# A linear-attention and MLP kernel on one core: 1 KB-run loads on one queue, casts on chip, streamed weights, a zero-padded last chunk and a ring of token tiles

## The chip, the cores and the metric

The kernel runs on one core of a Trainium2 chip. The core has TensorE (PE, matmuls and transposes into PSUM), VectorE (DVE), ScalarE (ACT), GpSimd (POOL) and SyncE (SP, which here issues DMAs). Sixteen DMA engines move data between HBM and SBUF. Each engine takes its own instructions in their order and waits on semaphores for the others. The metric is the device time of one execution in microseconds (us); lower is better.

## What is computed

Eight batches, eight heads, 576 tokens, head size 64. Attention without a score matrix, then a two-layer MLP over all 4608 tokens with the heads side by side (512 columns), all f32 in and out:

```python
q_s = softmax(q, axis=-1)                       # over the 64 values of a head
k_s = softmax(k, axis=2)                        # over the 576 tokens
kv  = einsum('bhsd,bhse->bhde', k_s, v)
x   = einsum('bhsd,bhde->bhse', q_s, kv)        # -> (4608, 512)
h   = x @ w_in                                  # (512, 2048)
out = maximum(0.01 * h, h) @ w_out              # (2048, 512)
```

## The kernel before

The Tile framework takes the program as it is written, gives each engine its list of instructions (in an order that its scheduler works out) and puts in the waits. All matmuls are bf16 with f32 sums.

**Loads.** `emit_loads(b)` cuts the 576 tokens of a batch into chunks of 128, 128, 128, 128 and 64, one token on each partition. For each chunk SP loads q and k (L107, L111) into `qk_sb` in f32: of each token and head one run of 64 values, 256 bytes. GpSimd loads v (L119) and casts it to bf16 on the way, two DMAs a chunk, into `v_sb`, with a column of ones beside it. GpSimd also loads and casts the weights: `w_in` in 16 pieces behind batch 0's v (L88), `w_out` in 8 behind batch 1's (L96).

**Attention of a batch** is a list of pieces. A prep piece for each chunk: ScalarE's exponential of q and k together (`qke_sb`, L135), DVE's row sums, reciprocal and scaling of q (`qsum` L138, `qrecip` L140, `qn_sb` L143). A transpose piece for each chunk: four PE transposes (`psum_qt`, L163) and DVE's copy into `qT_stage` (L171). Four `kv` pieces, one for each pair of heads: five matmuls (`pkv`, L186), a reciprocal (L194) and two scalings into the block-diagonal `kd_all` (L195, L202). Four out pieces: two matmuls of 288 columns (`po`, L218) and ScalarE's copies into `xT` (L225), one large tile for all 4608 tokens.

**MLP.** `emit_moe(t, pieces)` works on 512 tokens, nine token tiles in all. First 16 groups of four matmuls (`ph`, L251), each evicted by ScalarE with the leaky ReLU into `g_sb` (L259). Then four groups of 16 matmuls (`pout`, L277), each copied by DVE into `out_sb` (L285) and stored by SP (L287). After each group one attention piece of the next batch is put in, so that tile t carries the attention of batch t + 1 (tiles 0 to 6; 7 and 8 carry none). Token tile 0 lies within batch 0, tile 1 within batches 0 and 1. PSUM has 8 banks: six for `psB_pool` (all but `pout`), two for `pout`.

Of the kernel before, what the change touches and what calls it, by code (L numbers as in the profile page):

```python
# [19 lines left out]
def kernel(  # L21
# [22 lines left out]
    HEADS_PER_G = 2  # L44

    n_full = S // P
    rem = S - n_full * P
    chunk_sizes = [P] * n_full + ([rem] if rem else [])
    n_chunks = len(chunk_sizes)
# [43 lines left out]
    def emit_w_out_loads():  # L93
        w_out_r = moe_w_out.rearrange("(fb f) o -> f fb o", f=P)
        for fb0 in range(0, NF, 2):
            nc.gpsimd.dma_start(  # L96
                out=w_out_sb[:, fb0 : fb0 + 2, :], in_=w_out_r[:, fb0 : fb0 + 2, :]
            )

    xT = xT_pool.tile([P, NB, T], BF16)  # L100

    def emit_loads(b):
        st = {"qk": [], "v": [], "qke": {}, "qn": {}}
        for ci, cs in enumerate(chunk_sizes):
            s0 = ci * P
            qk_sb = qk_pool.tile([P, 2, H, D], FP32, name="qk_sb")
            nc.sync.dma_start(  # L107
                out=qk_sb[:cs, 0],
                in_=q[b, :, s0 : s0 + cs, :].rearrange("h s d -> s h d"),
            )  # L110
            nc.sync.dma_start(  # L111
                out=qk_sb[:cs, 1],
                in_=k[b, :, s0 : s0 + cs, :].rearrange("h s d -> s h d"),
            )

            v_sb = v_pool.tile([P, NG, 132], BF16, name="v_sb")
            v_src = v[b, :, s0 : s0 + cs, :].rearrange("(g hp) s d -> s g hp d", hp=2)
            for hp in range(HEADS_PER_G):
                nc.gpsimd.dma_start(  # L119
                    out=v_sb[:cs, :, hp * D : (hp + 1) * D],  # L120
                    in_=v_src[:, :, hp, :],
                )
# [219 lines left out]
```

## Time and profile before

| | us |
|---|---|
| median of 3 runs (348.08 to 349.3) | 349.28 |
| profiled execution, from its first to its last instruction | 346.2 |
| PE busy in it | 285.7 |
| ScalarE busy | 143.9 |
| DVE busy | 121.2 |
| GpSimd busy | 79.6 |

The profile is one execution. Its span leaves out what lies around the instructions; the run's time holds it. A busy time adds up the instructions of an engine. Matmuls are pipelined: one of 512 columns is listed with some 380 ns, but the next starts 216 ns after it. In the view by stage, a row is the stage, its length, the busy time (and instructions) of PE, of PE's weight loads, of DVE, ACT and POOL, then the TensorE clock as a share of full speed, the mean number of DMA engines' queues busy as a share of the 16 engines, and the GB/s that they moved. A row of a timeline is start, length, engine, line, operation, written tile and read tiles, number of instructions, and in brackets how long the engine had been idle and what ended that. In the DMA view a queue's row is packets, MB, and the packets' time as a share of 16 engines over the stretch. In the view by group a row is line, engine, operation, tiles, shapes and count, then busy us in all and mean ns of one, then idle time before them and its causes.

### The profile page before, as it was taken

The page shows a single profiled execution, that of the slowest core. Times are in us where ns is not written, and L with a number is a line of the kernel's source. Part 1 is how long each engine was busy: PE and PEld are TensorE (multiplying, and loading weights), DVE is VectorE, ACT ScalarE, POOL GpSimd, SP SyncE. Part 2 cuts the span into 40 slices and gives each one's busy share as a digit, 9 for nine tenths or more (in the row PEclk, how much of TensorE's full clock was granted, in tenths as well). Part 3 has the DMA queues.
Part 4 walks back from the last instruction along what each step waited for, and adds up shares of the span by engine and source line. Part 5 has one row for each costly group of instructions (what it writes and reads, how often), then busy time and mean ns, then how long its engine had stood idle before and what let it go on. Part 6 is the DMA issues. An engine that isn't in the chain of part 4 may idle for free.

```text
span 346.2 us, 4150 instructions
## 1 busy us (share of the span) xinstructions
PE 285.7 (83%) x1506; PEld 138.5 (40%) x1536; DVE 121.2 (35%) x292; ACT 143.9 (42%) x250; POOL 79.6 (23%) x158
## 2 busy tenths in 40 slices
PE   0203000999999999999999999999999999999995
PEld 0102000444445445544554454455445544444442
DVE  0523213476424822561465247225313210011011
ACT  2212111679155716753581457166225405503600
POOL 8667746208101700440071012000000000000000
PEclk9999999999999999999999999999999999999999
DMA  9999999999997992398089204100110021011011
GB/s 159 198 196 170 198 192 174 174 199 158 186 241 112 165 245 57 28 218 218 1 97 228 79 2 54 62 31 0 61 62 0 2 80 42 2 61 62 2 55 66
DMA packets 122837, 37.51 MB, mean 108 GB/s; under 512 B 114112, under 2 KB 118208, under 8 KB 122816
## 3 DMA queue, kind: packets, MB, share of 16 engines
q1 hardware_dynamic: 80192, 28.32, 38.0%
q0 software_dynamic: 42624, 8.92, 28.7%
q8 instruction: 12, 0.20, 0.2%
q14 instruction: 9, 0.07, 0.1%
HBM read 36.70 MB, written 9.44 MB: 133 GB/s over the span
## 4 chain that ended last, share of the span: by engine, by line
PE 78%; SPq 11%; DMA 8%; issue 1%; ACT 1%; DVE 0%; ACTq 0%
PE pout L277 36%; PE ph L251 35%; DMA qk_sb<-in_k_dram 8%; SPq L107 6%; SPq L111 5%; PE pkv L186 3%; PE psum_qt L163 2%; PE po L218 2%; ACT qke_sb L135 1%; DVE out_sb L285 0%; ACT g_sb L259 0%; ACTq L135 0%
## 5 line engine op out<-in xcount | busy, mean ns | idle before, releaser
L251 PE MATMUL ph<-xT,w_in_sb 128*128 128x512 bf16 x555 | 137.5, 382 | 2.0 <-ACT g_sb L259 0.7
L259 ACT ACTIVATE g_sb<-ph 128x512 bf16<-128x512 f32 x144 | 85.6, 598 | 113.4 <-PE ph L251 113.3
L277 PE MATMUL pout<-w_out_sb,g_sb 128*128 128x512 bf16 x567 | 127.6, 379 | 0.5
L119 POOL DMA_DIRECT2D v_sb<-in_v_dram x80 | 58.3, 749 | 113.1 <-PE pkv L186 102.2
L277 PEld LDWEIGHTS <-g_sb 128*128 128x128 bf16 x576 | 56.3, 98 | 64.1
L251 PEld LDWEIGHTS <-w_in_sb 128*128 128x128 bf16 x576 | 52.7, 98 | 55.7 <-issue 2.2
L135 ACT ACTIVATE qke_sb<-qk_sb 128x1024 bf16<-128x1024 f32 (+1 forms) x40 | 40.8, 1062 | 46.3 <-DMA qk_sb<-in_k_dram 46.3
L285 DVE COPY out_sb<-pout 128x512 f32<-128x512 f32 x36 | 24.6, 684 | 100.0 <-PE pout L277 83.2
L138 DVE TENSOR_REDUCE qsum<-qke_sb 128x8 f32<-128x512 bf16 (+1 forms) x40 | 26.8, 669 | 54.4 <-ACT qke_sb L135 54.2
L163 PE MATMUL psum_qt<-ident,qn_sb 128*128 128x128 bf16 (+1 forms) x160 | 15.7, 224 | 26.9 <-DVE qn_sb L143 26.9
L218 PE MATMUL po<-qT_stage,kd_all 128*128 128x288 bf16 x64 | 13.9, 304 | 27.1 <-DVE kd_all L202 27.0
L171 DVE COPY qT_stage<-psum_qt 128x512 bf16<-128x512 bf16 (+1 forms) x40 | 15.7, 396 | 43.8 <-PE psum_qt L163 43.4
L225 ACT CAST xT<-po 128x288 bf16<-128x288 f32 x64 | 22.2, 412 | 20.0 <-PE po L218 20.0
L143 DVE TENSOR_TENSOR qn_sb<-qke_sb,qrecip 128x512 bf16<-128x512 bf16 (+1 forms) x40 | 27.4, 686 | 0.8
L163 PEld LDWEIGHTS <-qn_sb 128*128 128x128 bf16 (+1 forms) x160 | 11.4, 101 | 37.5 <-DVE qn_sb L143 28.0
L218 PEld LDWEIGHTS <-kd_all 128*128 128x128 bf16 x64 | 6.1, 100 | 35.2 <-issue 27.2
L186 PE MATMUL pkv<-v_sb,qke_sb 128*128 128x129 bf16 (+1 forms) x160 | 18.5, 232 | 0.0
L186 PEld LDWEIGHTS <-qke_sb 128*128 128x128 bf16 (+1 forms) x160 | 13.0, 100 | 10.8 <-issue 0.8
L194 DVE RECIPROCAL krecip<-pkv 128x1 f32<-128x1 f32 x32 | 5.4, 168 | 20.0 <-PE pkv L186 20.0
L88 POOL DMA_DIRECT2D w_in_sb<-in_moe_w_in_dram x16 | 8.5, 535 | 5.0 <-DMA w_in_sb<-in_moe_w_in_dram 2.4
L202 DVE TENSOR_SCALAR kd_all<-pkv,krecip 64x64 bf16<-64x64 f32 x32 | 9.3, 291 | 0.5
L195 DVE TENSOR_SCALAR kd_all<-pkv,krecip 64x64 bf16<-64x64 f32 x32 | 8.8, 276 | 1.6
(12 smaller groups left out, 26.9 us busy)
## 6 DMA issues: line engine op xcount, KB each, us to landing
out_dram<-out_sb SPq DMA_DIRECT2D x36, 256.0 KB, 2.0
qk_sb<-in_q_dram SPq DMA_DIRECT2D x32, 256.0 KB, 5.2
qk_sb<-in_k_dram SPq DMA_DIRECT2D x32, 256.0 KB, 6.2
v_sb<-in_v_dram POOLq DMA_DIRECT2D x64, 64.0 KB, 6.1
w_in_sb<-in_moe_w_in_dram POOLq DMA_DIRECT2D x16, 128.0 KB, 6.5
w_out_sb<-in_moe_w_out_dram POOLq DMA_DIRECT2D x8, 256.0 KB, 10.2
qk_sb<-in_q_dram SPq DMA_DIRECT2D x8, 128.0 KB, 4.6
qk_sb<-in_k_dram SPq DMA_DIRECT2D x8, 128.0 KB, 4.5
```

Of the source, the lines that this page charges most:

```text
L119: nc.gpsimd.dma_start(out=v_sb[:cs, :, hp * D : (hp + 1) * D], in_=v_src[:, :, hp, :],)
L135: nc.scalar.activation(out=qke_sb[:cs], in_=qk_sb[:cs], func=AF.Exp)
L138: nc.vector.reduce_sum(out=qsum[:cs], in_=qke_sb[:cs, 0], axis=AX.X)
L143: nc.vector.tensor_tensor(out=qn_sb[:cs], in0=qke_sb[:cs, 0], in1=qrecip[:cs].to_broadcast([cs, H, D]), op=ALU.mult,)
L163: nc.tensor.matmul(psum_qt[:, j, 0:cs], lhsT=qn_flat[:cs, j * P : (j + 1) * P], rhs=ident[:cs, :cs], is_transpose=True, start=(j == 0), st ...
L186: nc.tensor.matmul(pkv[:, 0:129], lhsT=ke_flat[:cs, g * P : (g + 1) * P], rhs=st["v"][ci][:cs, g, 0:129], start=(ci == 0), stop=(ci == n_c ...
L218: nc.tensor.matmul(po[:, 0:width], lhsT=kd_all[:, g, :], rhs=qT_stage[:, g, lo : lo + width], start=True, stop=True,)
L225: nc.scalar.copy(out=xT[:, g, b * S + lo : b * S + lo + width], in_=po[:, 0:width])
L251: nc.tensor.matmul(ph, lhsT=w_in_sb[:, cb, j * P : (j + 1) * P], rhs=xT[:, cb, t0 : t0 + TT], start=(cb == 0), stop=(cb == NB - 1),)
L259: nc.scalar.activation(out=g_sb[:, j, :], in_=ph, func=AF.Prelu, alpha=LEAKY_SLOPE)
L277: nc.tensor.matmul(pout, lhsT=g_sb[:, j, tsub * P : (tsub + 1) * P], rhs=w_out_sb[:, j, :], start=(j == 0), stop=(j == NF - 1),)
L285: nc.vector.tensor_copy(out=out_sb, in_=pout)
```

## The change

- **Loads.** SP issues every load, all in f32. A batch's first 512 tokens are dealt out four neighbours to a partition (R = 4), so that a partition reads of each head one run of 4 x 64 values, 1 KB (L95); the last 64 tokens (REM) go in runs of 256 bytes to 64 partitions (L99). q, k and v each have one staging tile of a ring of 8 (`ld`). Token order inside the 512 is undone when ScalarE writes `xT`.
- **Casts.** The weights come in quarters of 1 MB through the same ring, and DVE casts them (L121, L126). v is cast by ScalarE for batch 0 and by DVE for the others (L156, L157).
- **Order.** Batch 0 in halves, `w_in`, three quarters of `w_out`, batch 1, the last quarter of `w_out`, then batch 2 and on.
- **Zero-padded last chunk.** The buffers for exponentials and v (`qe`, `ke`, `vb`, two of each) are fixed tiles; their unused 64 partitions of the fifth chunk are set to zero once, so that every matmul has 128 rows. GpSimd does nothing but build the identity.
- **Attention.** Exponentials and softmax by halves of the heads; two pairs of heads to a `pkv` tile; `po` as 512 + 64 columns, the 64 copied by DVE. Batch 0 multiplies k and v ahead of the transposes.
- **Tiles.** `xT` is a ring of three token tiles. All PSUM tiles share 8 banks. Tile 0 takes no piece during `ph`, and its four `pout` sums run side by side, each weight row of `w_out` used for all four; pieces come in from its ninth row on.

```diff
-    xT_pool = ctx.enter_context(tc.tile_pool(name="xT", bufs=1))
-    qk_pool = ctx.enter_context(tc.tile_pool(name="qk", bufs=8))
...
+    ld_pool = ctx.enter_context(tc.tile_pool(name="ld", bufs=8))
+    xT_pool = ctx.enter_context(tc.tile_pool(name="xT", bufs=3))
+    ps_pool = ctx.enter_context(tc.tile_pool(name="ps", bufs=8, space=bass.MemoryType.PSUM))
...
+    def load_rows(dst, src, b, h0, h1):
+        nc.sync.dma_start(
+            out=dst[:, h0:h1, 0 : R * D],
+            in_=src[b, h0:h1, 0:MAIN, :].rearrange("h (p r) d -> p h (r d)", r=R),
+        )
+        nc.sync.dma_start(
+            out=dst[0:REM, h0:h1, R * D : NR * D],
+            in_=src[b, h0:h1, MAIN:S, :].rearrange("h p d -> p h d"),
+        )
...
-                nc.gpsimd.dma_start(
-                    out=w_in_sb[:, cb, fq * FQ : (fq + 1) * FQ],
-                    in_=w_in_r[:, cb, fq * FQ : (fq + 1) * FQ],
-                )
+    def emit_w_in(i):
+        stg = ld_pool.tile([P, NB, FQ], FP32, name="w_in_ld", tag="ld")
+        nc.sync.dma_start(out=stg, in_=w_in_r[:, :, i * FQ : (i + 1) * FQ])
+        nc.vector.tensor_copy(out=w_in_sb[:, :, i * FQ : (i + 1) * FQ], in_=stg)
...
+            copy = nc.scalar.copy if b == 0 else nc.vector.tensor_copy
+            copy(out=vb[:, 0:R, h0:h1, 0:D], in_=rhd(st["v"][:, h0:h1, 0 : R * D], R))
+            copy(out=vb[0:REM, R, h0:h1, 0:D], in_=st["v"][0:REM, h0:h1, R * D : NR * D])
...
+        if b == 0:
+            front = [make_exp(st, b, "q", 0), make_exp(st, b, "q", 1)]
+            front += [make_qnorm(st, b, 0), make_qnorm(st, b, 1)]
+            for hf in range(2):
+                front += [make_exp(st, b, "k", hf), make_vcast(st, b, hf), make_kv(st, b, hf)]
...
+        if t == 0:
+            pouts = [
+                ps_pool.tile([P, O], FP32, name="pout", tag=BANK) for _ in range(NTS)
+            ]
             for j in range(NF):
...
+                for tsub in range(NTS):
+                    gemm2_mm(pouts[tsub], g_sb, tsub, j)
+                if pieces and j >= 8:
+                    pieces.pop(0)()
+            for tsub in range(NTS):
+                store(pouts[tsub], t, tsub)
...
-    batch_state[0] = emit_loads(0)
-    emit_w_in_loads()
-    batch_state[1] = emit_loads(1)
-    emit_w_out_loads()
...
+    for i in range(WQ):
+        emit_w_in(i)
+    for piece in attn_pieces(0, states[0]):
+        piece()
+    for i in range(WQ - 1):
+        emit_w_out(i)
+    states[1] = emit_loads(1, whole)
+    emit_w_out(WQ - 1)
```

What stands in a row on the engines is shown at three places. First DVE, before, between the last transposes of batch 0 and the scalings that fill its `kd_all` (`qke_sb_380` and `qke_sb_422` are the first and fourth chunk of batch 1):

```order
L171 COPY qT_stage_241<-psum_qt_266 128x4x64
L194 RECIPROCAL krecip_280<-pkv_274 128x1
...
L138 TENSOR_REDUCE qsum_382<-qke_sb_380 128x8
L194 RECIPROCAL krecip_310<-pkv_304 128x1
L140 RECIPROCAL qrecip_384<-qsum_382 128x8
L143 TENSOR_TENSOR qn_sb_386<-qke_sb_380,qrecip_384 128x512
...
L138 TENSOR_REDUCE qsum_424<-qke_sb_422 128x8
L140 RECIPROCAL qrecip_426<-qsum_424 128x8
L143 TENSOR_TENSOR qn_sb_428<-qke_sb_422,qrecip_426 128x512
L195 TENSOR_SCALAR kd_all_272<-pkv_274,krecip_280 64x64
L202 TENSOR_SCALAR kd_all_272<-pkv_274,krecip_280 64x64
```

and the same place now (`w_in_ld_126` is the first quarter of `w_in`, the `po2` are batch 0's, `qe1` belongs to batch 1):

```order
L219 TENSOR_TENSOR kd0_92<-pkv_181,krec_192 64x2x64 x2
L196 COPY qT_196<-pt_203 128x4x128
...
L196 COPY qT_196<-pt_215 128x4x128
L121 CAST w_in_sb_109<-w_in_ld_126 128x4x512
L196 CAST qT_196<-pt_221 128x4x64
L257 CAST xT_233<-po2_229 128x64
...
L121 CAST w_in_sb_109<-w_in_ld_129 128x4x512
...
L126 CAST w_out_sb_110<-w_out_ld_259 128x2048
L169 TENSOR_REDUCE qsum_426<-qe1_99 128x16
```

Batch 1's softmax has moved behind all of batch 0 and behind the casts of the weights, and a cast that waits for a load stands ahead of batch 0's last `qT` copy.

Second SP, before, from the program's start, where it issues q and k of batch 0 and then of batch 1 (`qk_sb_158` on), while GpSimd issues the rest:

```order
L107 DMA qk_sb_107<-in_q_dram 128x8x64
L111 DMA qk_sb_107<-in_k_dram 128x8x64
...
L107 DMA qk_sb_135<-in_q_dram 64x8x64
L111 DMA qk_sb_135<-in_k_dram 64x8x64
L107 DMA qk_sb_158<-in_q_dram 128x8x64
```

and now, from the end of batch 0 on (`q_ld_262`, `k_ld_263`, `v_ld_264` are batch 1's, `q_ld_274` batch 2's):

```order
L95 DMA v_ld_113<-in_v_dram 128x4x256
L99 DMA v_ld_113<-in_v_dram 64x4x64
L120 DMA w_in_ld_126<-in_moe_w_in_dram 128x4x512
...
L125 DMA w_out_ld_259<-in_moe_w_out_dram 128x4x512
L95 DMA q_ld_262<-in_q_dram 128x8x256
L99 DMA q_ld_262<-in_q_dram 64x8x64
L95 DMA k_ld_263<-in_k_dram 128x8x256
...
L95 DMA v_ld_264<-in_v_dram 128x8x256
...
L125 DMA w_out_ld_271<-in_moe_w_out_dram 128x4x512
L95 DMA q_ld_274<-in_q_dram 128x8x256
```

The loads of v and of the weights have moved from GpSimd's queue into this one.

Third DVE, now, at the end of tile 0 (`vb1`, `kd1` and `qT_518` are batch 1's, `qe0` is batch 2's by then, `pout_380` tile 0's first sum):

```order
L156 CAST vb1_101<-v_ld_264 128x4x4x64 x2
L157 CAST vb1_101<-v_ld_264 64x4x64 x2
L217 RECIPROCAL krec_499<-pkv_488 128x2
L219 TENSOR_TENSOR kd1_102<-pkv_488,krec_499 64x2x64 x2
...
L196 COPY qT_518<-pt_525 128x4x128
L126 CAST w_out_sb_110<-w_out_ld_271 128x2048
...
L196 CAST qT_518<-pt_543 128x4x64
L169 TENSOR_REDUCE qsum_602<-qe0_89 128x16
L291 COPY out_sb_476<-pout_380 128x512
```

The cast of v, the last quarter of `w_out` and a sum of batch 2 have come in among the steps that tile 1 needs; before, no cast stood on DVE.

## Rows read from the trace of the kernel before

**Rows 1.** The page: the span, and PE's busy time.
```profile
span 346.2 us, 4150 instructions
PE 285.7 (83%) x1506; PEld 138.5 (40%) x1536; DVE 121.2 (35%) x292; ACT 143.9 (42%) x250; POOL 79.6 (23%) x158
```

**Rows 2.** Busy time by stage: three of the ramp, tile 0, tiles 2 to 6.
```profile
0.00:10.00 10.00, 0.43 (x4) 0.34 (x4) 1.69 (x4) 3.49 (x4) 9.01 (x23) 1.00 1.21 162
10.00:20.00 10.00, 1.39 (x10) 0.69 (x8) 4.14 (x9) 1.06 (x1) 6.01 (x12) 1.00 1.45 200
...
40.00:50.00 10.00, 0.00 (x0) 0.00 (x0) 1.00 (x3) 0.49 (x1) 5.08 (x10) 1.00 1.21 196
...
62.10:96.00 33.90, 32.78 (x173) 15.91 (x176) 18.48 (x46) 20.08 (x37) 8.87 (x19) 1.00 1.17 180
...
127.80:286.80 159.00, 158.05 (x863) 77.84 (x880) 62.70 (x157) 75.35 (x137) 19.40 (x39) 1.00 0.38 73
```

**Rows 3.** Timeline of PE: batch 0's sums, then where token tiles start.
```profile
29.66 3.13 PE L186 MATMUL pkv<-v_sb,qke_sb 128*128 128x129 bf16 x20
...
59.82 2.52 PE L218 MATMUL po<-qT_stage,kd_all 128*128 128x288 bf16 x8 [27.03 <-DVE kd_all L202]
62.13 1.49 PE L251 MATMUL ph<-xT,w_in_sb 128*128 128x512 bf16 x3
63.84 2.47 PE L251 MATMUL ph<-xT,w_in_sb 128*128 128x512 bf16 x9 [0.22 <-issue]
...
96.03 1.24 PE L251 MATMUL ph<-xT,w_in_sb 128*128 128x512 bf16 x5
...
127.83 0.81 PE L251 MATMUL ph<-xT,w_in_sb 128*128 128x512 bf16 x3
...
286.83 0.81 PE L251 MATMUL ph<-xT,w_in_sb 128*128 128x512 bf16 x3
...
314.46 0.81 PE L251 MATMUL ph<-xT,w_in_sb 128*128 128x512 bf16 x2
```

**Rows 4.** Timeline of ScalarE and DVE, 49 to 60 us.
```profile
49.51 1.06 ACT L135 ACTIVATE qke_sb<-qk_sb 128x1024 bf16<-128x1024 f32 x1 [10.12 <-DMA qk_sb<-in_k_dram]
...
56.44 1.06 ACT L135 ACTIVATE qke_sb<-qk_sb 128x1024 bf16<-128x1024 f32 x1 [5.88 <-DMA qk_sb<-in_k_dram]
...
59.10 0.27 DVE L195 TENSOR_SCALAR kd_all<-pkv,krecip 64x64 bf16<-64x64 f32 x1
```

**Rows 5.** DMA queues, 1.9 to 3.7 us; 40 to 48 us; 337.0 to 337.7 us.
```profile
q1 hardware_dynamic: 1641, 0.42, 101.7%
...
q0 software_dynamic: 1283, 1.24, 91.2%
...
q1 hardware_dynamic: 130, 0.24, 91.6%
```

**Rows 6.** The page, DMA issues: count, KB each, median us to landing.
```profile
out_dram<-out_sb SPq DMA_DIRECT2D x36, 256.0 KB, 2.0
```

**Rows 7.** Groups by line and shape: busy us, mean ns of one.
```profile
L259 ACT ACTIVATE g_sb<-ph 128x512 bf16<-128x512 f32 x144 | 85.6, 598 | 113.4 <-PE ph L251 113.3
...
L135 ACT ACTIVATE qke_sb<-qk_sb 128x1024 bf16<-128x1024 f32 x32 | 32.8, 1059 | 38.6 <-DMA qk_sb<-in_k_dram 38.5
L285 DVE COPY out_sb<-pout 128x512 f32<-128x512 f32 x36 | 24.6, 684 | 100.0 <-PE pout L277 83.2 <-remote 16.6
...
L143 DVE TENSOR_TENSOR qn_sb<-qke_sb,qrecip 128x512 bf16<-128x512 bf16 x32 | 22.0, 687 | 0.5
L138 DVE TENSOR_REDUCE qsum<-qke_sb 128x8 f32<-128x512 bf16 x32 | 21.4, 667 | 42.4 <-ACT qke_sb L135 42.2
...
L171 DVE COPY qT_stage<-psum_qt 128x512 bf16<-128x512 bf16 x32 | 13.3, 422 | 39.3 <-PE psum_qt L163 39.0
...
L140 DVE RECIPROCAL qrecip<-qsum 128x8 f32<-128x8 f32 x32 | 6.4, 199 | 0.5
...
L171 DVE COPY qT_stage<-psum_qt 128x256 bf16<-128x256 bf16 x8 | 2.3, 290 | 4.4 <-PE psum_qt L163 4.4
```

More of the change, by code (lines that the diff above doesn't have):

```diff
@@ L43 @@
     NG = H // 2
[L44 to L49, printed above, removed]
+    VW = D + 2
+    R = S // P
+    MAIN = R * P
+    REM = S - MAIN
+    NR = R + 1
+    assert 0 < REM <= P and REM % 32 == 0
     TT = 512
@@ L93, in emit_w_out_loads @@
[L93 to L97, printed above, removed]
-            )
[L100 to L122, printed above, removed]
-            nc.gpsimd.memset(v_sb[:, :, 128:129], 1.0)
-            st["qk"].append(qk_sb)
-            st["v"].append(v_sb)
-        return st
@@ L212, in make_out_piece @@
-    def make_out_piece(b, st, g):
-        def piece():
-            kd_all = st["kd"]
-            qT_stage = st["qT"]
-            for lo, width in ((0, 288), (288, 288)):
-                po = psB_pool.tile([P, 288], FP32, name="po", tag=BANK_TAG)
-                nc.tensor.matmul(
-                    po[:, 0:width],
-                    lhsT=kd_all[:, g, :],
-                    rhs=qT_stage[:, g, lo : lo + width],
-                    start=True,
-                    stop=True,
-                )
-                nc.scalar.copy(
-                    out=xT[:, g, b * S + lo : b * S + lo + width], in_=po[:, 0:width]
-                )
-        return piece
@@ L231, in make_attn_pieces @@
[L231 to L243 removed]
+            ke, vb, kd = ke_buf[b % 2], v_buf[b % 2], kd_buf[b % 2]
@@ new lines, in piece @@
+            pkv = ps_pool.tile([P, 2, 2 * VW], FP32, name="pkv", tag=BANK)
+            for i in range(2):
+                g = gp * 2 + i
+                for r in range(NR):
+                    nc.tensor.matmul(
+                        pkv[:, i, 0 : VW + D],
+                        lhsT=ke[:, r, g * P : (g + 1) * P],
+                        rhs=vb[:, r, 2 * g : 2 * g + 2, :].rearrange("p h e -> p (h e)")[:, 0 : VW + D],
+                        start=(r == 0),
+                        stop=(r == NR - 1),
+                    )
@@ new lines, in piece @@
+            krec = small_pool.tile([P, 2, 1], FP32, name="krec")
+            nc.vector.reciprocal(out=krec, in_=pkv[:, :, D : D + 1])
+            for lo, at in ((0, 0), (64, VW)):
+                nc.vector.tensor_tensor(
+                    out=kd[lo : lo + 64, gp * 2 : gp * 2 + 2, lo : lo + 64],
+                    in0=pkv[lo : lo + 64, :, at : at + D],
+                    in1=krec[lo : lo + 64].to_broadcast([64, 2, 64]),
+                    op=ALU.mult,
+                )
+        return piece
@@ new lines, in gemm2_mm, with store, emit_moe @@
+    def gemm2_mm(pout, g_sb, tsub, j):
+        nc.tensor.matmul(
+            pout,
+            lhsT=g_sb[:, j, tsub * P : (tsub + 1) * P],
+            rhs=w_out_sb[:, j, :],
+            start=(j == 0),
+            stop=(j == NF - 1),
+        )
+    def store(pout, t, tsub):
+        out_sb = osb_pool.tile([P, O], FP32, name="out_sb")
+        nc.vector.tensor_copy(out=out_sb, in_=pout)
+        r0 = t * TT + tsub * P
+        nc.sync.dma_start(out=out[r0 : r0 + P, :], in_=out_sb)
+    def emit_moe(t, pieces):
```

298 lines of the change are left out of this document (160 added, 138 removed).

## The prediction

> **What bounds the kernel now.** I read the page first, then the engines by stage, then the start of each token tile on TensorE (PE), and last what the other engines do before that start. PE is busy 285.7 of 346.2 us [rows 1]. The stages are not alike [rows 2]. From 127.8 to 286.8 us PE is busy 158.05 of 159.00 us: nothing on another engine can make that stretch shorter. From 40 to 50 us it does nothing while the DMA engines are full at 196 GB/s. So there are two regimes: a ramp that waits for loads, and a steady part in which PE is the limit.
>
> The first matmuls of the token tiles give the measure [rows 3]. Tile 0 starts at 62.13 us, tile 1 at 96.03, tile 2 at 127.83, tile 7 at 286.83, tile 8 at 314.46. A tile with a batch's attention among its matmuls takes (286.83 - 127.83)/5 = 31.80 us, one without takes 27.63, so attention costs PE 4.17 us a batch. Tile 0 takes 33.90. Everything behind 96.03 us is 250.2 us of PE at full pace, and the change removes no matmul. **So the question is when tile 1 starts.**
>
> Why is tile 0 so late? PE has done batch 0's last attention sums at 32.8 us (29.66 + 3.13) and then waits 27.0 us [rows 3]. VectorE (DVE) takes its instructions in order; the scalings that fill `kd_all` for batch 0 stand behind four softmax groups of batch 1, and these wait for ScalarE's exponentials, which wait 10.12 and 5.88 us for the loads of `k` of batch 1 [rows 4]. Tile 0 thus waits for most of batches 0 and 1 and for all weights, over DMA engines that are busy all the time at 162 to 200 GB/s (the least and the most of the 10 us stages before 60 us, both in [rows 2]).
>
> **The change, part by part.** *Packets.* The time of one packet on one DMA engine is share x 16 engines x stretch / packets [rows 5]. 256 bytes: 1.017 x 16 x 1.8/1641 = 17.8 ns. A weight read of 2 KB: 0.912 x 16 x 8.0/1283 = 91 ns. A stored 2 KB: at most 0.916 x 16 x 0.7/118 = 87 ns (0.24 MB are 118 packets). No row shows a read of 1 KB. It lies between half of 87 (43) and four of 17.8 (71); on the straight line from 17.8 to 91 it takes 49 ns, and that I use (334 GB/s), since the same engines show both ends.
> Of q, k or v of one batch, each DMA engine now reads 64 packets of 1 KB (partition x head, 1024/16) and 32 of 256 bytes for the 64 left-over tokens: 64 x 49 + 32 x 17.8 = 3.7 us a tensor, 11.1 us a batch. A quarter of `w_in` or `w_out` is 32 packets of 2 KB: 2.9 us.
>
> *One queue.* All loads now stand in SP's order: batch 0, four `w_in`, three `w_out`, batch 1, the last `w_out`, batch 2. A store of 256 KB lands 2.0 us after issue [rows 6], of which its 8 packets per engine are 0.7, so 1.3 is fixed; with the first issue at 0.7 us a load lands at 2.0 + the transfers up to it. Batch 0: 13.1. `w_in` quarters: 16.0, 18.9, 21.8, 24.7. Third `w_out`: 33.4. q, k, v of batch 1: 37.1, 40.8, 44.5. Fourth `w_out`: 47.4. q of batch 2: 51.1. The staging ring of 8 makes some loads wait for a cast; the tightest is k of batch 1 behind the cast of the first `w_in`, which is done (20.4, below) well before the queue gets there (37). So the queue does not run dry.
>
> *Casts on chip.* DVE gains eight casts of 2048 f32 elements and, per batch, casts of v (2 x 1024, 2 x 256). No row shows an f32 copy from SBUF on DVE. The f32 copy from PSUM takes 684 ns for 512 [rows 7], four of them 2.7 us; the bf16 copy's slope, (422 - 290)/256 = 0.52 ns an element, gives 1.2. I take 2.2 (the f32 row's pace, its fixed part paid once), 1.2 for 1024 and 0.4 for 256. Three such steps lie on the path below, so the lower end would be worth some 3 us. The Trainium skill, VectorE: DVE Perf Modes, section "The perf-mode tier table", gives an f32 copy within SBUF double rate, 1.23 us for 2048; no row here shows it, and by it the sum would come to 315 us. The twelve memsets at the start run while q loads; at 0.5 us each they end at 6, as ScalarE's first exponentials do.
>
> *Tile 0's start.* The last half of v lands at 13.1; ScalarE copies it (1024 elements 1.06 [rows 7], 256 elements 0.4): 14.6. Six `pkv` sums at 0.155 each (3.13/20, [rows 3]): 15.5. Fifteen transposes at about the same: 17.8. The last `qT` copy, 0.42: 18.2. Now DVE stands at the cast of the first `w_in` (landed 16.0): 20.4. Left-over `qT` cast, 0.3: 20.7. First `po`, 0.6: 21.3. Four ScalarE copies of 512 at 0.6 (the evictions of [rows 7] have 512 in 598 ns): 23.7. **Tile 0 starts at 24 instead of 62.1.** The other quarters of `w_in` land ahead of their use, 3.45 us apart (16 x 0.216).
>
> *Tile 1's start.* The `ph` sums and three quarters of `pout` are 112 matmuls at 0.216 = 24.2 us, and 1.2 for the low clock at the start: 49.4. The rows for that clock: three matmuls take 1.49 us from 62.13, five 1.24 from 96.03 [rows 3], so 0.43 apart and then 0.215, half rate (1.2 GHz) and full rate (2.4). The windows print 1.00 for both and are no guide there. ScalarE's exponentials of batch 1 stand behind all 16 evictions of tile 0: 39.6. DVE's softmax of batch 1 (four rows of 1.2, four of 0.4, reciprocals at 0.2, from [rows 7]) runs from 40.7 to 48, its casts of v to 51.0. So PE waits 1.6 us for v, does the rest of `pkv` and `pt` (3 us, 54.0), and DVE, with `kd`, two copies and the last `w_out` cast, frees the last quarter of `pout` at 56.7. That is 16 matmuls: 60.2. Then the `po` sums, all bunched: first 0.4, then four pairs of ScalarE copies (0.55 + 0.25): 63.8. **Tile 1 starts at 64 instead of 96: 32 us less.** ScalarE's exponentials of batch 2, which it takes before these copies, need q at 51.1 and 3.0 us: 54, covered.
>
> *After that.* The matmuls of a batch are as many as before (20 + 20 + 8) and ScalarE has some 19 us of work in the 31.8 (16 evictions at 0.6, exponentials 5.8, copies 3.2), DVE no more. I add 0.1 us a tile for wider `po` and `pkv`, 0.7 in all. The 1 KB loads, three 1.18 MB tensors a tile, take 11 us of 32.
>
> **The sum.** The profiled execution spans 346.2 us; the runs' median is 349.28, 3.1 us around the span. 349.3 - 32.0 + 0.7 = **318 us**.
>
> **The rivals.** *The clock falls in the ramp's waits.* After 27.0 us without work PE ran at half rate until about 64 [rows 3]; I charged one such start. PE now waits at the `pkv` of batch 1 and again before tile 1. If each wait brings the low clock back, each costs what tile 0 paid over tile 2, 33.90 - 31.80 = 2.1: 322 us. Against it: these waits are 1.6 to 3.6 us, not 27. The Trainium skill's page TensorE: Matmul & The Clock Gate, section "HAM oscillation", says that PE gaps from DMA waits do send it back; the 27 us row agrees, none here shows a short one.
>
> *Loads slower than the line.* At 71 ns per 1 KB, q of batch 2 lands at 60.9, tile 1 starts at 67.5: 321. If all loads together give 250 GB/s, 16.65 MB end at 68.6 and exponentials and copies (6.6) follow: tile 1 at 75, 329.
>
> *Slower than before.* If the 190 or so GB/s of the ramp is no matter of packet size but what one core gets (the 10 us windows never pass 200), f32 staging through one queue gains nothing: q of batch 2 at 2.0 + 16.65/0.190 = 89.6, tile 1 at 96.2, no gain, about 350. That is the point from which it decides; at 162 GB/s tile 1 starts at 111, 365 us. Against it: 231 GB/s with 256-byte packets alone, and 91 ns for 2 KB, 360 GB/s [rows 5].
>
> *The steady part begins to wait.* Loads and stores now share SP's order: v of batch 4 is issued behind the stores of tile 1 and is needed by DVE some 3 us after it lands; behind DVE's casts stand the `krec`, `kd` and `out_sb` work for which PE and its banks wait. If each of tiles 1 to 5 loses 2 to 3 us: 328 to 333.
>
> **How the numbers follow.** Forecast, 309 to 326: 0.68. Low clock, 322 (inside it): 0.10. Loads at 250: 0.06. Steady waits: 0.10. No gain at 190 GB/s: 0.02; slower: 0.04. The range 309 to 333 leaves out the last two and the far tail of the loads. About 0.5% is what a measurement here can tell from no change: faster 0.94, same 0.02, slower 0.04.
>
> **What would show it.** Right: the first `ph` at 22 to 26 us and the first of tile 1 at 60 to 68; 1 KB packets at 43 to 55 ns; tiles from 1 on 31.8 us apart. Wrong: DMA below 250 GB/s up to 50 us; PE idle before `pkv` for 5 us or more in tile 0; idle PE in tiles 1 to 6 that ends on a DVE cast of v or an exponential; half-rate matmuls behind 30 us.

## The result and the profile after

The changed kernel takes 311.7 us (median; 310.32 to 312.88) against 349.29 (348.08 to 349.84): a ratio of 0.8937, 95% interval 0.8898 to 0.8975. The forecast was 318, range 309 to 333. The sign, the range and the main mechanism hold; two terms of the sum were wrong, and a rival that I gave 0.10 came true in part.

The page of the changed kernel (busy us, share of the span, instructions; the granted clock in 40 slices; the queue's packets, MB and share of 16 engines; then a group as in [rows 7]):

```profile
span 310.9 us, 3915 instructions
...
PE 282.6 (91%) x1536; PEld 136.8 (44%) x1536; DVE 131.4 (42%) x300; ACT 167.1 (54%) x274; POOL 0.7 (0%) x6
...
PEclk9996999979999999999999999999999999999999
...
q1 hardware_dynamic: 47136, 46.14, 50.7%
...
L249 ACT CAST xT<-po 128x448 bf16<-128x448 f32 (+7 forms) x60 | 40.8, 821 | 38.2 <-PE po L240 4.1
```

Against [rows 1], PE's busy time is nearly the same, 282.6 us for 285.7; the span is 35.3 us shorter, and almost all of that is idle time of PE. ScalarE has become busier (167.1 us for 143.9): its copies into `xT`, 60 at a mean of 821 ns, come back below. `PEclk` shows two dips, near 30 and near 65 us.

The token tiles on PE (start, length, engine, line, operation, tiles, count, idle before), to be read against [rows 3]:

```profile
24.45 0.38 PE L302 MATMUL ph<-xT,w_in_sb 128*128 128x512 bf16 x1
25.48 17.24 PE L302 MATMUL ph<-xT,w_in_sb 128*128 128x512 bf16 x63 [0.66 <-ACT xT L249]
42.56 10.52 PE L281 MATMUL pout<-w_out_sb,g_sb 128*128 128x512 bf16 x48
52.92 0.62 PE L209 MATMUL pkv<-vb_101,ke_100 128*128 128x130 bf16 x8
...
57.69 3.61 PE L281 MATMUL pout<-w_out_sb,g_sb 128*128 128x512 bf16 x16 [1.31 <-DVE w_out_sb L126]
61.14 0.38 PE L240 MATMUL po<-qT,kd_102 128*128 128x512 bf16 x1
...
62.90 0.19 PE L242 MATMUL po_566<-qT,kd_102 128*128 128x64 bf16 x1 [0.89 <-ACT xT L249]
...
64.03 0.19 PE L242 MATMUL po_573<-qT,kd_102 128*128 128x64 bf16 x1 [0.73 <-ACT xT L249]
65.16 0.81 PE L302 MATMUL ph<-xT,w_in_sb 128*128 128x512 bf16 x3 [0.94 <-ACT xT L249]
...
98.00 7.93 PE L302 MATMUL ph<-xT,w_in_sb 128*128 128x512 bf16 x36
...
251.75 1.46 PE L302 MATMUL ph<-xT,w_in_sb 128*128 128x512 bf16 x6
```

Tile 1 starts at 65.16 us where it started at 96.03: 30.9 us earlier. Tile 1 then takes 32.84, and tiles 2 to 6 take (251.75 - 98.00)/5 = **30.75 us each, not 31.80**. The span's account is thus 30.9 at the ramp, minus 1.0 for tile 1, plus 5 x 1.05 for tiles 2 to 6, and 0.2 at the end: 35.3.

The stages (start and end, length, busy time of PE, PE's weight loads, DVE, ACT, POOL, then granted clock, DMA share, GB/s), against [rows 2]:

```profile
0.00:10.00 10.00, 0.00 (x0) 0.00 (x0) 4.77 (x17) 4.10 (x6) 0.70 (x6) 1.00 0.79 217
...
20.00:30.00 10.00, 7.11 (x34) 3.19 (x33) 7.94 (x15) 6.10 (x6) 0.00 (x0) 0.76 1.05 387
...
25.00:32.00 7.00, 6.24 (x15) 1.99 (x15) 4.48 (x4) 4.52 (x6) 0.00 (x0) 0.51 1.04 387
66.00:70.00 4.00, 3.84 (x11) 1.37 (x11) 4.00 (x10) 3.10 (x7) 0.00 (x0) 0.57 0.74 229
98.00:251.70 153.70, 153.70 (x881) 75.83 (x880) 63.75 (x157) 88.05 (x148) 0.00 (x0) 1.00 0.41 114
```

Where the old ramp never passed 200 GB/s in any of these stages, the new one reaches 387 while it reads only weights in 2 KB packets. The clock stood at half (0.51) from 25 to 32 us, and for most of 66 to 70 us (0.57). From 98 to 251.7 us PE does not pause at all.

The two rates do not count the same thing, though. The queues of the kernel before, on its page, and what both kernels read:

```profile
q1 hardware_dynamic: 80192, 28.32, 38.0%
q0 software_dynamic: 42624, 8.92, 28.7%
...
HBM read 36.70 MB, written 9.44 MB: 133 GB/s over the span
```

SP's queue (q1) holds q, k and the stores. GpSimd's (q0) brought v and the weights, 17.83 MB of f32, and is listed with 8.92, half of that: a load that casts is counted by the bf16 that it writes. (The one queue of the changed kernel lists 46.14 MB, all of 36.70 + 9.44.) In the first 60 us the old queues list 5.08 MB (q1) and 5.95 (q0), so 5.08 + 2 x 5.95 = 17.0 MB were read, 283 GB/s; now it is 18.46 MB, 308 GB/s. The same 17.0 MB at the new rate would take 55 us, so by this estimate reading faster is some 5 us of the ramp's 30.9. That leaves most of it to what is read first and to what stands behind it on the engines.

### The profile page after: what moved, and what is told of

It is laid out like the page before. It is cut to its first block, busy times and chain, and to the rows that moved or that the text cites. A ratio compares the mean times of both kernels' runs of the same rounds, so it can differ in the third digit from the quotient of the medians.

```text
span 310.9 us, 3915 instructions
## 1 busy us (share of the span) xinstructions
PE 282.6 (91%) x1536; PEld 136.8 (44%) x1536; DVE 131.4 (42%) x300; ACT 167.1 (54%) x274; POOL 0.7 (0%) x6
## 3 DMA queue, kind: packets, MB, share of 16 engines
q1 hardware_dynamic: 47136, 46.14, 50.7%
HBM read 36.70 MB, written 9.44 MB: 148 GB/s over the span
## 4 chain that ended last, share of the span: by engine, by line
PE 88%; ACT 3%; SPq 3%; DMA 3%; DVE 3%; issue 0%
PE ph L302 41%; PE pout L281 40%; PE pkv L209 3%; ACT xT L249 3%; DMA v_ld<-in_v_dram 3%; PE pt L188 2%; PE po L240 2%; SPq L99 2%; SPq L95 1%; DVE qT L196 1%; DVE w_out_sb L126 0%; DVE w_in_sb L121 0%; DVE kd_102 L219 0%; ACT vb_91 L156 0%; DVE out_sb L291 0%
## 5 line engine op out<-in xcount | busy, mean ns | idle before, releaser
L249 ACT CAST xT<-po 128x448 bf16<-128x448 f32 (+7 forms) x60 | 40.8, 821 | 38.2 <-PE po L240 4.1
L209 PE MATMUL pkv<-vb_91,ke_90 128*128 128x130 bf16 x80 | 7.0, 242 | 16.9 <-ACT vb_91 L156 16.9
L196 DVE COPY qT<-pt 128x512 bf16<-128x512 bf16 x32 | 13.0, 422 | 8.9 <-PE pt L188 8.5
L138 ACT ACTIVATE qe_89<-q_ld 128x1024 bf16<-128x1024 f32 x8 | 8.4, 1059 | 14.1 <-DMA q_ld<-in_q_dram 14.1
L169 DVE TENSOR_REDUCE qsum<-qe_99 128x16 f32<-128x1024 bf16 (+1 forms) x16 | 12.4, 783 | 6.8 <-ACT qe_99 L138 6.8
L169 DVE TENSOR_REDUCE qsum<-qe_89 128x16 f32<-128x1024 bf16 (+1 forms) x16 | 12.5, 787 | 4.4 <-ACT qe_89 L138 4.4
L217 DVE RECIPROCAL krec<-pkv 128x2 f32<-128x2 f32 x16 | 2.7, 170 | 27.3 <-PE pkv L209 27.2
L209 PEld LDWEIGHTS <-ke_90 128*128 128x128 bf16 x80 | 6.1, 108 | 18.4 <-ACT ke_90 L138 12.8
L171 DVE TENSOR_TENSOR qe_99<-qe_99,qrec 128x1024 bf16<-128x1024 bf16 (+1 forms) x16 | 12.8, 804 | 0.1
L171 DVE TENSOR_TENSOR qe_89<-qe_89,qrec 128x1024 bf16<-128x1024 bf16 (+1 forms) x16 | 12.8, 807 | 0.1
L138 ACT ACTIVATE ke_90<-k_ld 128x1024 bf16<-128x1024 f32 x8 | 8.5, 1062 | 3.3 <-DMA k_ld<-in_k_dram 3.3
L156 DVE CAST vb_91<-v_ld 128x1024 bf16<-128x1024 f32 x6 | 4.0, 682 | 12.2 <-DMA v_ld<-in_v_dram 12.2
L156 DVE CAST vb_101<-v_ld 128x1024 bf16<-128x1024 f32 x8 | 5.3, 684 | 8.2 <-PE pkv L209 7.6
L138 ACT ACTIVATE ke_100<-k_ld 128x1024 bf16<-128x1024 f32 x8 | 8.3, 1063 | 0.0
L138 ACT ACTIVATE qe_99<-q_ld 128x1024 bf16<-128x1024 f32 x8 | 8.3, 1047 | 0.0
L188 PEld LDWEIGHTS <-qe_89 128*128 128x128 bf16 x80 | 6.6, 111 | 3.5
```

The costliest lines, as they stand in the source:

```text
L138: nc.scalar.activation(out=dst[:, 0:R, h0 * D : h1 * D].rearrange("p r (h d) -> p r h d", d=D), in_=rhd(src[:, h0:h1, 0 : R * D], R), func ...
L156: copy(out=vb[:, 0:R, h0:h1, 0:D], in_=rhd(st["v"][:, h0:h1, 0 : R * D], R))
L169: nc.vector.reduce_sum(out=qsum[0:p1, r0:r1, :], in_=x, axis=AX.X)
L171: nc.vector.tensor_tensor(out=x, in0=x, in1=qrec[0:p1, r0:r1, :].unsqueeze(3).to_broadcast([p1, r1 - r0, HH, D]), op=ALU.mult,)
L188: nc.tensor.matmul(pt[:, j, :], lhsT=qe_buf[b % 2][:, r, j * P : (j + 1) * P], rhs=ident[:, 0:n], is_transpose=full, start=(j == 0) or not ...
L196: nc.vector.tensor_copy(out=st["qT"][:, :, r * P : r * P + n], in_=pt)
```

## The experiments

Eight kernels ran, each an edit of the changed kernel except the last, which edits the kernel before. The kernel before, run beside them, took 347.8 and 348.5 us on their chips.

**The last chunk at 64 rows again.** Is the shorter steady tile the zero padding?

```diff
-                    lhsT=qe_buf[b % 2][:, r, j * P : (j + 1) * P],
-                    rhs=ident[:, 0:n],
+                    lhsT=qe_buf[b % 2][0:n, r, j * P : (j + 1) * P],
+                    rhs=ident[0:n, 0:n],
...
-                        lhsT=ke[:, r, g * P : (g + 1) * P],
+                        lhsT=ke[0 : (P if r < R else REM), r, g * P : (g + 1) * P],
...
```

> The changed kernel with one thing undone: the matmuls of the last chunk take its 64 real rows only (kv sums and transposes), as before, and the zero rows are not read. The order on every engine stays. Theory: the 64-row weights make TensorE pause, and this alone is the 1.05 us by which a tile with attention became shorter (31.80 to 30.75): tiles 2 to 6 are 31.7 to 31.9 us apart again, the whole is 6 to 8 us longer than the changed kernel, about 319 us. Rival: the saving came from ten kv sums in a row in place of five, or from other waits: tiles stay at 30.75 and the time at 312.

Measured: 319.0 us, ratio 0.9152 (0.9113 to 0.9191). Tiles 2 to 6 are 31.80 us apart again. The steady tile's PE timeline in the changed kernel, and then in this one:

```profile
105.77 0.73 PE L209 MATMUL pkv<-vb_101,ke_100 128*128 128x130 bf16 x10
106.34 1.03 PE L302 MATMUL ph<-xT,w_in_sb 128*128 128x512 bf16 x4
...
112.98 0.28 PE L188 MATMUL pt<-ident,qe_99 128*128 128x64 bf16 x4
113.09 0.59 PE L302 MATMUL ph<-xT,w_in_sb 128*128 128x512 bf16 x2
```

```profile
105.55 1.04 PE L209 MATMUL pkv<-vb,ke 128*128 128x130 bf16 x10
106.53 1.04 PE L304 MATMUL ph<-xT,w_in_sb 128*128 128x512 bf16 x4
...
113.69 0.29 PE L188 MATMUL pt<-ident,qe 64*128 64x64 bf16 x4
113.92 1.04 PE L304 MATMUL ph<-xT,w_in_sb 128*128 128x512 bf16 x4
```

What counts is the time to the next row's start. Ten `pkv` sums take 106.34 - 105.77 = 0.57 us with the fifth chunk padded, and 0.98 with it at 64 rows, though the number of sums is the same: 0.41 more for a group that has two such sums. With two groups a batch that is 0.82. The last four transposes take 0.11 us when padded and 0.23 when not, and the four `ph` ahead of them 0.86 (from 112.12) and 0.96 (from 112.73): together 1.04 of the 1.05. Four 64-row transposes in a row thus cost 0.22 us more, as much as one lone 64-row sum (0.41 for two): by these rows it is the change from 128 rows to 64 and back that costs, some 0.1 us each way, and not each short matmul. So the zeros, which add arithmetic and no result, pay back about 1 us a tile, some 7 us in the run (319.0 against 311.7).

**256-byte runs.** The order stays; every run is of 64 values again. (`main(dst)` is the same staging tile, laid out so that the runs lie side by side.)

```diff
-            out=dst[:, h0:h1, 0 : R * D],
-            in_=src[b, h0:h1, 0:MAIN, :].rearrange("h (p r) d -> p h (r d)", r=R),
+            out=main(dst)[:, h0:h1, :].rearrange("p h (r d) -> p (h r) d", r=R),
+            in_=src[b, h0:h1, :, :].rearrange("h (r t) d -> t (h r) d", r=R)[0:P],
```

> The changed kernel with q, k and v read in runs of 256 bytes in place of 1 KB, in as many DMAs, on the same queue, in the same order and bytes; the first 512 places hold other tokens of the batch than the reference puts there (tokens 144 r + p), so the output has tokens in the wrong places. Theory, as predicted: packet size sets the rate. 256 packets a tensor and engine at 17.8 ns are 4.6 us in place of 64 at 49 = 3.1, so 4.3 us more a batch; v of batch 1 and q of batch 2 land 9 to 10 us later, tile 1 starts 7 to 10 us later, 319 to 322 us. Rival: the 1 KB packets were slowed to 60 to 69 ns by the 256-byte packets beside them, so little is lost: tile 1 at most 3 us later, 312 to 315 us. Third: other things than the rate of loads set tile 1: no change.

Measured: 318.61 us, ratio 0.9146 (0.9109 to 0.9183). Its queue from 6 to 9 us, in which all packets are of 256 bytes:

```profile
DMA packets 2392, 0.60 MB, mean 201 GB/s; under 512 B 2392, under 2 KB 2392, under 8 KB 2392
...
q1 hardware_dynamic: 2392, 0.60, 127.6%
```

That is 1.276 x 16 x 3/2392 = 25.6 ns a packet and 201 GB/s. Tile 0 starts at 28.32 and tile 1 at 69.62, 4.5 us later than in the changed kernel. Run length is worth some 7 us: nearer the theory than the rival, and just short of the theory. The later loads, of whole tensors, ran at 199 GB/s from 40 to 50 us, against 302 in the changed kernel, although the trace lists most of their packets at 1024 bytes, with some 80 ns each from 30 to 60 us where the changed kernel's have 60. So the run that the program writes down isn't always the packet that moves, and the size of the packet alone does not set its price.

**Without the left-over tokens' loads.** The other way round: the 256-byte packets go, and GpSimd writes zeros in their place.

```diff
-        nc.sync.dma_start(
-            out=dst[0:REM, h0:h1, R * D : NR * D],
-            in_=src[b, h0:h1, MAIN:S, :].rearrange("h p d -> p h d"),
-        )
+        nc.gpsimd.memset(dst[0:REM, h0:h1, R * D : NR * D], 0.0)
```

> The changed kernel without the loads of the 64 left-over tokens (the 256-byte packets); GpSimd fills their places with zeros, so these tokens are left out of the computation. Theory: the small packets slow the 1 KB packets beside them; alone these take 46 to 50 ns in place of 60 to 69, batch 0 lands at 11 to 12 us in place of 16.7, tile 0 starts at 19 to 21, tile 1 at 59 to 62 us: 305 to 308 us. Rival: the small packets cost their own time alone, 1.7 us a batch: 1 KB packets stay above 55 ns and tile 0 starts at 22.5 or later.

Measured: 309.1 us, ratio 0.8876 (0.8857 to 0.8895). The queue from 6 to 9 us in the changed kernel, and then in this one:

```profile
DMA packets 1130, 0.82 MB, mean 274 GB/s; under 512 B 422, under 2 KB 1130, under 8 KB 1130
...
q1 hardware_dynamic: 1130, 0.82, 111.5%
```

```profile
DMA packets 1020, 1.01 MB, mean 338 GB/s; under 512 B 29, under 2 KB 1020, under 8 KB 1020
...
q1 hardware_dynamic: 1020, 1.01, 102.3%
```

Almost alone, a packet takes 1.023 x 16 x 3/1020 = 48 ns: the straight line's 49. In the mixture, the 422 short ones at the 17.8 ns of [rows 5] take 7.5 of 53.5 us, which leaves 65 ns for each of the 708 packets of 1 KB. So the short packets slow the long ones beside them. The time gained was smaller than expected, 2.6 us: tile 0 came 2.4 us earlier (22.1) and tile 1 2.9 (62.27). ScalarE now takes the last half of v at 14.18, straight after its exponentials and without waiting for the load, so that its own list sets the start of batch 0's sums; and the waits for the copies into `xT` and the second low clock stayed (2.40 us before tile 1, which took 32.8).

**A dense write of `xT`.** Only the order in which ScalarE walks its copy: the jumps are on the PSUM side now, and SBUF is written in memory order.

```diff
-                    out=xT_of(t)[:, g, o0 : o0 + hi - lo].rearrange("c (p r) -> c r p", r=R),
-                    in_=src[:, :, lo // R : hi // R],
+                    out=xT_of(t)[:, g, o0 : o0 + hi - lo].rearrange("c (p r) -> c p r", r=R),
+                    in_=src[:, :, lo // R : hi // R].rearrange("c r p -> c p r"),
```

> The changed kernel with the copy into the token tile walking its output in memory order (the stride of four lies on the PSUM side, not on the SBUF side); the rest and its order stay. Theory: the strided write doubled ScalarE's copy (512 columns took 1.2 us where 0.6 was expected), so the copy goes back to 0.6 us, tile 0 starts 2 us earlier and tile 1 some 3.5 us earlier than in the changed kernel, and with a shorter pause before tile 1 the clock may not fall: 306 to 309 us. Rival: a stride costs the same on the PSUM side: copies stay at 1.2 us and the time at 312.

Measured: **306.81 us, ratio 0.8814 (0.8753 to 0.8876)**, 1.4% under the changed kernel. One shape of the copy (busy us, mean ns) in the changed kernel, and in this one:

```profile
L249 ACT CAST xT<-po 128x448 bf16<-128x448 f32 x8 | 9.3, 1213 | 3.1 <-PE po_551 L242 3.1
```

```profile
L249 ACT CAST xT<-po 128x448 bf16<-128x448 f32 x8 | 4.3, 538 | 0.0
```

The same 448 elements take 1213 ns when written with a stride of four and 538 when written densely. PE's way into tile 1 in this kernel:

```profile
58.19 0.38 PE L240 MATMUL po<-qT,kd 128*128 128x512 bf16 x1 [0.26 <-DVE out_sb L291]
...
58.79 0.38 PE L240 MATMUL po<-qT,kd 128*128 128x512 bf16 x1 [0.18 <-DVE out_sb L291]
...
59.50 1.24 PE L302 MATMUL ph<-xT,w_in_sb 128*128 128x512 bf16 x5 [0.30 <-ACT xT L249]
```

The waits of 0.89, 0.73 and 0.94 us have become 0.26, 0.18 and 0.30 (the first two for DVE's `out_sb` copies), and in this execution the clock does not fall before tile 1, which takes 30.85 us instead of 32.84. Tile 1 starts 5.7 us earlier; of that, about 1.8 lies in the last step (61.14 to 65.16 is 4.0, here 57.28 to 59.50 is 2.2). The rest lies ahead of it, and not all of that is the edit's: with the same loads, the last half of v was there at 15.35 us and not at 17.09, and the clock, once up at 25.7, stayed up, where the changed kernel's profile has it low until 32.0. The profiled execution is the fastest of four here (305.2; the slowest is 309.53) and the slowest of four there (312.88), so the medians, 4.9 us apart, are the better measure.

**The rest of batch 1 ahead of the last quarter of `pout`.** So that PE has matmuls while the copies run.

```diff
             for j in range(NF):
+                if j == 12:
+                    while pieces:
+                        pieces.pop(0)()
                 for tsub in range(NTS):
```

> The changed kernel with tile 0's remaining pieces (the transposes and po sums of batch 1) put ahead of the last quarter of the pout sums in place of behind it. Theory: the last 16 pout matmuls (3.5 us) then cover ScalarE's copies into the token tile, TensorE does not pause for 4 us before tile 1, and the clock stays at its higher level: tile 1 starts 3 to 4 us earlier and takes 30.8 in place of 32.8 us: 305 to 308 us. Rival: the last w_out cast or the kd scalings on VectorE end last anyway, tile 1 starts no earlier, and the time stays at 310 to 312.

Measured: 307.92 us, ratio 0.8828 (0.8784 to 0.8872). Tile 1 starts at 62.62 and takes 30.99. The scheduler mixes the `po` sums with the last `pout` matmuls, and one wait for `xT`, 0.52 us, is left where there were three. A low clock is there all the same, but from 55.83 to 59.24 us, ahead of tile 1. Of the 2.5 us by which tile 1 starts earlier, 1.85 lie ahead of the edited code (the last quarter of `pout` starts at 55.84, against 57.69); what the edit gives shows from there to the start of tile 2, 37.8 us in place of 40.3. PE's way into tile 1:

```profile
60.66 0.19 PE L242 MATMUL po<-qT,kd 128*128 128x64 bf16 x1 [0.52 <-ACT xT L249]
60.69 2.10 PE L281 MATMUL pout<-w_out_sb,g_sb 128*128 128x512 bf16 x9
62.62 0.59 PE L302 MATMUL ph<-xT,w_in_sb 128*128 128x512 bf16 x2
```

**Both of these.**

```diff
+                if j == 12:
+                    while pieces:
+                        pieces.pop(0)()
...
+                    out=xT_of(t)[:, g, o0 : o0 + hi - lo].rearrange("c (p r) -> c p r", r=R),
+                    in_=src[:, :, lo // R : hi // R].rearrange("c r p -> c p r"),
```

> The changed kernel with both of the edits that helped, the dense write of the token tile and batch 1's remaining pieces ahead of the last pout quarter. Theory: they shorten the same stretch between pout and tile 1, so the gains do not add up: tile 1 starts at 56 to 58.5 us, tiles from 1 on 30.75 apart: 302 to 305 us. Rival: nothing beyond the dense write alone, 306 to 307 us.

Measured: 306.58 us, ratio 0.8808 (0.8787 to 0.883): the dense write alone, within the intervals. They remove the same wait only in part. From the start of the last quarter of `pout` to tile 1 it is 4.5 us here (55.93 to 60.43), against 5.7 with the dense write alone (53.83 to 59.50) and 7.5 in the changed kernel (57.69 to 65.16). What takes this gain lies ahead of it. DVE and then PE in this kernel:

```profile
49.57 1.30 DVE L156 CAST vb<-v_ld 128x1024 bf16<-128x1024 f32 x2 [1.91 <-DMA v_ld<-in_v_dram]
```

```profile
50.32 0.39 PE L209 MATMUL pkv<-vb,ke 128*128 128x130 bf16 x4 [2.61 <-DVE vb L156]
...
55.93 1.02 PE L281 MATMUL pout<-w_out_sb,g_sb 128*128 128x512 bf16 x4 [1.27 <-DVE w_out_sb L126]
```

Tile 0 has become so early that it waits for v of batch 1, through DVE's cast; the wait that the prediction had placed at this point of the changed kernel appears here, and the clock falls behind it (51.1 to 54.5 us). The dense write alone waits there too, less: its cast of v starts at 47.94, 1.04 us after DVE was free.

**The weights by GpSimd again.** They are cast on the way, in a second queue, and DVE casts no weights. With that the scheduler also puts batch 1's pieces behind all of tile 0's `pout`.

```diff
-        stg = ld_pool.tile([P, NB, FQ], FP32, name="w_in_ld", tag="ld")
-        nc.sync.dma_start(out=stg, in_=w_in_r[:, :, i * FQ : (i + 1) * FQ])
-        nc.vector.tensor_copy(out=w_in_sb[:, :, i * FQ : (i + 1) * FQ], in_=stg)
+        for cb in range(NB):
+            nc.gpsimd.dma_start(
+                out=w_in_sb[:, cb, i * FQ : (i + 1) * FQ],
+                in_=w_in_r[:, cb, i * FQ : (i + 1) * FQ],
+            )
...
```

> The changed kernel with the weights loaded as before, cast on the way by GpSimd's queue from the start (24 DMAs), without VectorE's casts; q, k and v stay on SP's queue. Batch 1's attention then stands behind all of tile 0's pout sums. Theory: both queues share the 16 DMA engines, so batch 0 lands some 5 to 9 us later (at 22 to 26), tile 0 starts at 29 to 32 and tile 1 at 66 to 70: 313 to 318 us, slower than the changed kernel. Rival: the one queue brings nothing, since the engines move the same bytes either way and VectorE is spared 9.8 us of casts: 308 to 312 us.

Measured: 330.54 us, ratio 0.948 (0.945 to 0.9509): a far greater loss than either side expected. Its queues from 2 to 30 us, its last copy of batch 0's v on ScalarE, and its start of tile 0:

```profile
q0 software_dynamic: 3322, 3.09, 67.6%
q1 hardware_dynamic: 4316, 3.27, 44.4%
```

```profile
34.26 1.04 ACT L159 CAST vb<-v_ld 128x1024 bf16<-128x1024 f32 x1 [3.78 <-DMA v_ld<-in_v_dram]
```

```profile
44.51 1.86 PE L305 MATMUL ph<-xT,w_in_sb 128*128 128x512 bf16 x4 [2.61 <-ACT xT L252]
```

In the changed kernel the same copy of v starts at 17.09. Both queues draw on the same engines: while the weights move, SP's queue has 44.4% of their time and batch 0 lands 17 us later. The engines read no less than before: the 3.09 MB of q0 are 6.18 MB of f32, with the 3.27 of q1 337 GB/s, against 325 (9.11 MB) in the changed kernel from 2 to 30 us. So what is lost is the order of arrival and not the rate. One queue in the order of need is worth about 19 us (330.5 - 311.7), more than any other part that was taken out alone; the moved pieces of batch 1 are within that, and no run takes them out.

**The old kernel in the new order.** The kernel before; only the order in the program is changed, and tile 0 takes no piece during `ph`.

```diff
-            if pieces:
+            if pieces and t > 0:
                 pieces.pop(0)()
...
-    batch_state[1] = emit_loads(1)
-    emit_w_out_loads()
     for piece in make_attn_pieces(0, batch_state[0]):
         piece()
+    emit_w_out_loads()
+    batch_state[1] = emit_loads(1)
```

> The kernel before with its order alone changed: batch 0's attention is written ahead of the w_out and batch 1 loads, and tile 0 takes no piece of batch 1 during its ph groups. Loads keep their 256-byte runs, their two queues and GpSimd's casts. Theory: tile 0 waited for VectorE and ScalarE, which stood behind batch 1's loads, more than for bytes; it now starts at 33 to 37 us, tile 1 at 69 to 75, 322 to 328 us. So most of the gain does not come from faster loads. Rival: the loads at some 195 GB/s set tile 1 all the same (batch 1 and the weights land at 56 to 63 us and batch 1's attention follows): tile 1 at 80 to 88, 335 us or more.

Measured: 337.74 us, ratio 0.9699 (0.9675 to 0.9722), tile 1 at 86.85: as the rival had it. PE and ScalarE before tile 0:

```profile
43.60 0.70 PE L218 MATMUL po<-qT_stage,kd_all 128*128 128x288 bf16 x2 [7.06 <-ACT xT L225]
```

```profile
42.21 1.06 ACT L135 ACTIVATE qke_sb<-qk_sb 128x1024 bf16<-128x1024 f32 x1 [11.91 <-DMA qk_sb<-in_k_dram]
```

The wait on DVE that [rows 3] shows is gone, but an exponential of batch 1 stands ahead of ScalarE's copies for batch 0 and waits 11.91 us for its load. The queues still list 182 and 196 GB/s in the first two 20 us (by bytes read 286 over the first 60 us). The program's order alone is worth 11 us. What is left is not the total that the engines read: with two queues side by side SP's brings q and k at only 5.11 MB in 60 us, 85 GB/s, and on these the exponentials wait.

These sizes don't add up to the whole (7 for padding, 7 for run length, 19 for the queue): each was taken with the others in place, and in the ramp they share waits.

## Why the prediction came out as it did

**The mechanism was right.** I said that the question was when tile 1 starts, and that the ramp would be worth 32 us; it was worth 30.9. The rival in which one core gets no more than some 190 GB/s is refuted by 387 GB/s from 20 to 30 us. Its figure was a misreading, as was "full at 196 GB/s": both count GpSimd's casting loads at half of what they read (351 GB/s from 40 to 50 us: 0.41 MB of q1 and twice 1.55 of q0). So less of the time won lies in faster reading than 190 against 334 GB/s would suggest, and more in the order.

**Inside the ramp, errors of both signs met.** From the timelines:

| step | predicted us | measured us |
|---|---|---|
| last half of v of batch 0 landed | 13.1 | 17.1 |
| DVE cast of 2048 | 2.2 | 1.23 |
| ScalarE copy of 512 into `xT` | 0.6 | 1.36 |
| tile 0 running | 24 | 25.5 |
| `ph` and three quarters of `pout` | 25.4 | 27.4 |
| wait before `pkv` of batch 1 | 1.6 | 0 |
| last quarter of `pout` done | 60.2 | 61.1 |
| from there to tile 1 | 3.6 | 4.0 |
| tile 1 starts | 64 | 65.16 |

Batch 0 landed 4 us late, because I gave each packet its own price and the short packets slowed the long ones (192 packets of 1 KB an engine at 65 in place of 49 ns are 3.1 us of it); the 217 GB/s of the first 10 us is one of the signs of "wrong" that I had named. Two things gave 2.5 us of it back. PE did not need all four copies into `xT`, as I had it: its first sums began with the first and ran on after the second; 1.4 us of this came back as waits inside `ph`, below. And DVE's casts were half as long:

```profile
22.07 1.23 DVE L121 CAST w_in_sb<-w_in_ld 128x2048 bf16<-128x2048 f32 x1
```

That is the value that the Trainium skill gives (VectorE: DVE Perf Modes, "The perf-mode tier table"); the trace agrees. I had charged the pace of the f32 copy that reads PSUM, which was the nearest row and the wrong one. The ScalarE copies erred the other way. I priced them by [rows 7], an eviction that writes densely, and did not ask in which order the new ones write; they took 1.36 us for 512:

```profile
61.55 4.71 ACT L249 CAST xT<-po 128x448 bf16<-128x448 f32 x8 [3.06 <-PE po_551 L242]
```

This row is the eight copies of batch 1, 4.71 us without a break where I had four pairs at 0.55 + 0.25 = 3.2; PE's three waits before 65.16 us end on them. (The memsets at the start, for which I had taken 0.5 us each without a row, took 0.07 to 0.28 and delayed nothing.)

**The clock rival came true in part.** I gave it 0.10 and argued that waits of 1.6 to 3.6 us are not 27. In the profiled execution, by the records of the clock, it fell to half (1.2 GHz) from 25.1 to 32.0 us and from 66.1 to 69.5 (the two short stages above), so half-rate matmuls behind 30 us, another sign that I had named, were there. The 63 `ph` matmuls took 17.1 us to the next row where 63 x 0.216 = 13.6 would do. Not all of the 3.5 us is the clock's. ScalarE's copies into `xT` for tile 0 end at 27.73:

```profile
24.13 3.60 ACT L249 CAST xT<-po 128x512 bf16<-128x512 f32 x3 [0.32 <-PE po_237 L242]
```

From 25.48 to 27.78 PE has only four matmuls that it can do, 0.9 us at full rate, so 1.4 us are the copies'. The other 59 take 14.8 us where 12.7 would do, so the clock cost 2.0; I had charged 1.2. The second dip made up some 1.7 of the 2.1 us by which tile 1 is longer than its successors; the rest is a wait for `xT` at 66.16. It came after waits of 1.31, 0.89, 0.73 and 0.94 us, each far shorter than 27. The Trainium skill's page TensorE: Matmul & The Clock Gate, section "HAM oscillation", names PE gaps from DMA waits as the cause; here the gaps came from a cast on DVE and copies on ScalarE.

Such waits do not settle it, though. In the 64-row kernel the same four were followed by a fall (64.9 to 68.3 us); in the 256-byte kernel, with 1.31, 0.67, 0.75 and 0.37, the profile shows none. The first stretch differs from profile to profile: the clock came up at 27.3 us in the 64-row kernel and at 25.7 with the dense write and stayed up, and here at 21.7, to fall again. Executions of one kernel differ as well: the four of the changed kernel have mean granted clocks of 0.984, 0.989, 0.994 and 0.994 over spans of 310.9, 310.6, 308.9 and 308.4 us, and the profile is of the first, so its two dips were not in every execution. What decides whether the clock falls is not settled by these runs.

**The step that failed is "after that".** I added 0.1 us a tile, 0.7 in all, "for wider `po` and `pkv`", having counted the matmuls of a batch, which are as many as before. Measured: minus 1.05 us for each of tiles 2 to 6, plus 1.0 for tile 1: minus 4.2. The first experiment shows that the count was right and the price was not: going from 128 rows to 64 and back between matmuls costs more time than full rows do. [Rows 3] held half of the sign: tiles with attention took 4.17 us more, and I did not split that over the 20 sums, 20 transposes and 8 `po`.

**A smaller term: the base.** I set the sum against the median, 349.3, and read the 3.1 us above the profiled span as what lies around it. The four runs of the changed kernel lie only 1.9 to 2.0 us above their own spans, and the fourteen of the kernel before beside the experiments 1.8 to 1.9; by that the profiled 346.2 goes with the run of 348.08. So of the 6.3 us between 318 and 311.7, the later tiles make 4.9 (0.7 + 4.2), the end 0.2 and the ramp -1.1, and 2.3 come from which runs were profiled: before, one 1.2 below its median, and now one 1.2 above (312.88), the one with the most low clock.

## What to carry to other kernels

Price a group of matmuls by the time from its start to the next group's start within the stage where it will run, and not by their number; where a tile has a short last chunk, zero-filling it to full rows may be cheaper than saving the rows. Before a rate from a profile is called a limit, ask whether a casting load is counted by what it reads or by what it writes. For a copy ask which side the stride is on, and take as its price a row of the same memory and the same write order. When waits on a load fall, look at the waits of a microsecond that are left before a long run of matmuls: they cost themselves, and the clock may fall behind them.
